# A quarter of one double weight tile loaded in fp32 over a second queue and cast on chip

## The chip, the cores and the metric

The kernel runs on one core of one Trainium2 chip. The time is device microseconds of a whole execution. The kernel before takes 436.98 us, the median of three runs (436.07 to 437.49).

The core has TensorE (PE; its weight loads are listed apart as PEld), VectorE (DVE), ScalarE (ACT), GpSimd (POOL) and SyncE (SP). Data moves between the chip's main memory and the on-chip memory of 128 partitions over 16 DMA engines, which are shared by the queues of SP and of POOL. A DMA issued from POOL's queue can change the type on the way (here fp32 to bf16); one issued from SP's queue moves the bytes as they are.

## The reference

Two layers follow one another. The first is a causal attention with a window of 128 and a bias that falls with distance, over 8 batches, 8 heads, 576 positions and 64 values a head. Its output `x` (8 x 576 x 512) goes into the second, which mixes in the spectrum:

```
X = np.fft.rfft(x, axis=1)
Xr, Xi = real and imaginary part of X[:, :64]
Yr = np.einsum('bmd,mde->bme', Xr, w_r) - np.einsum('bmd,mde->bme', Xi, w_i)
Yi = np.einsum('bmd,mde->bme', Xr, w_i) + np.einsum('bmd,mde->bme', Xi, w_r)
y = irfft of Y, which is zero outside the first 64 modes
u = x + y
out = u + np.maximum(u @ w_ch, 0.0)
```

For each of 64 modes there are two 512 x 512 fp32 matrices, one of `w_r` and one of `w_i`, of 1 MB each. Together they are most of what the kernel reads.

## The kernel before

**Two parts.** The first part (class `_Attention`) runs the attention of 16 units of one batch and four heads, in a fixed order of stages. While it runs, the first weights are fetched. The second part goes through the 64 modes in 16 groups `g` of four, and multiplies the eight batches' spectra (the stationary operand, columns of `XC`) with the modes' matrices (the moving operand, `wq`), L920. The order of the instructions of every engine is written out by hand: each engine does its work in the order in which the program emits it.

**Weights and turns.** A weight is numbered `i = 2 * mode + kind`, kind 0 for `w_r` and 1 for `w_i`. `turns` lists the order of use. Up to the last group a turn is two weights of the same kind and neighbouring modes, `[96, 98]` for example, which is `w_r` of modes 48 and 49. Of each matrix, partition `p` holds the four rows `4p` to `4p + 3`, which are 8 KB of fp32 in one run in main memory and become 4 KB of bf16 on chip.

**Loads.** All weights come over POOL's queue and are cast to bf16 by the DMA. The first 21, and eight more later, come one by one (`load_w`, L472). All others come as packs of two (`load_packs`). If both weights of the pack have the same kind, one DMA of 2 MB of fp32 brings them into a tile `[128, 2, 4, 512]` of bf16 (L491). In the last group a pack has both kinds of one mode, and comes in two or more DMAs (L499).

**Buffers and order.** Packs live in two pools of tiles with the tag `w`: the pool `w` with six buffers (`NWA // 2`) and, from position 40 on, the pool `w2` with two (`NWB // 2`). A pool hands its buffers out in rotation, and a load into a buffer waits until the matmuls that used it before are done. In the loop over `g` and `i`, the position is `k = 8 * g + i`. The position emits the eight matmuls of its turn (two weights by four row sets, L920), and after them the load of one more pack into the pool of the pack just used. Pack 96 and 98 is loaded after the turn at position 80 and used at position 96, the first of group 12. POOL issues its DMAs in order and waits before each for its buffer.

**Work beside it.** From group 8 on each position also emits a piece of side work: `project` (PE, with ACT's copies L715 and DVE's copy L692) or `augment` (PE, with a cast on ACT, L736, and one on DVE, L737). At the end of a group DVE scales the group's result (L608). After the last weight the kernel finishes the last modes and the token rows, and writes the output over SP's queue. Between 285 and 402 us SP issues no DMA.

Of the kernel before, what the change touches and what calls it, by code (L numbers as in the profile page):

```python
# [10 lines left out]
FP32 = mybir.dt.float32  # L11
BF16 = mybir.dt.bfloat16
# [8 lines left out]
P = 128  # L21
# [391 lines left out]
def kernel(  # L413
# [10 lines left out]
    nc = tc.nc  # L424
    ctx.enter_context(tc.manual_schedule(engines=ALL | {SP}))
    B, H, S, _ = q.shape
    NM, DM, _ = moe_w_r.shape
    AHEAD = {stage: 1 for stage in range(1, 14)}
    LATER = {12: 1, 13: 2, 14: 2, 15: 2}
    EARLY, NWA, NWB, AGAIN = 14, 12, 4, 8  # L430
    HM = NM // 2

    const = ctx.enter_context(tc.tile_pool(name="const", bufs=1))
    x = const.tile([P, B, FULL + 1, DM], BF16, name="x")
# [23 lines left out]
                      else [[2 * m], [2 * m + 1], [2 * m + 2], [2 * m + 3]])  # L458
    spot = {i: k for k, i in enumerate(i for turn in turns for i in turn)}
    turns[1].remove(1)  # L460
    wq, homes, todo_w, again = {}, {}, [i for turn in turns for i in turn], []

    def load_w(n, pool, chosen=None):
# [11 lines left out]
    def load_packs(n, pool):  # L475

        for _ in range(n):
            pack = [i for i in todo_w if i not in again][:2]
            if not pack:
                return  # L480
            assert len(pack) == 2
            t = pool.tile([P, 2, 4, DM], BF16, tag="w", name="w")
            kinds = {i % 2 for i in pack}
            for s, i in enumerate(pack):
                todo_w.remove(i)
                homes[i] = pool if s else False
                wq[i] = [t[:, s, a] for a in range(4)]
            m, w = pack[0] // 2, (moe_w_r, moe_w_i)
            if len(kinds) == 1:
                assert pack[1] == pack[0] + 2  # L490
                nc.gpsimd.dma_start(  # L491
                    out=t.rearrange("p s a e -> p s (a e)"),
                    in_=w[kinds.pop()][m : m + 2].rearrange("m (p a) e -> p m (a e)", a=4))
                continue
            for s, i in enumerate(pack):
                src = w[i % 2][i // 2].rearrange("(p a) e -> p a e", a=4)
                for part in ((slice(0, 4),) if i < 2 * NM - 1
                             else (slice(0, 2), slice(2, 3), slice(3, 4))):
                    nc.gpsimd.dma_start(out=t[:, s, part], in_=src[:, part])  # L499

    with ExitStack() as actx:
        at = _Attention(tc, actx, q, k, v, (ident, F, FT), x, XC, raw)
        n = len(at.units)
# [10 lines left out]
        pool = _Scratch(x[:, B - 2 :].rearrange("p b t c -> p (b t c)").bitcast(FP32))  # L514
# [55 lines left out]
    with ExitStack() as mctx:  # L570
        fix = mctx.enter_context(tc.tile_pool(name="fix", bufs=1))
        YT = fix.tile([P, 2, 4, B, HM, 2], BF16, name="YT")
        pool = mctx.enter_context(tc.tile_pool(name="fin", bufs=2))
        wctx = mctx.enter_context(ExitStack())
        wpool = wctx.enter_context(tc.tile_pool(name="w", bufs=NWA // 2, reuse_waits="tile"))
        again = todo_w[NWA : NWA + AGAIN]
        load_packs(NWA // 2, wpool)
        nc.gpsimd.memset(YT[:, 1, :, :, HM - 4 :], 0.0)
        lctx, pctx = ExitStack(), ExitStack()
# [261 lines left out]
        def finish_tokens(j):  # L841

            late_modes(yys[j][0], j, Z)
# [52 lines left out]
        for g in range(NM // 4):  # L896
# [5 lines left out]
            for i in range(8):  # L902
                k = 8 * g + i
                if i == 6 and g == LAST:
# [7 lines left out]
                    add_tokens(0)  # L912
                    finish_tokens(0)
                now = turns.pop(0) if turns and spot[turns[0][0]] == k else []
                for a in range(4):
                    for t in now:
                        m, ri = t // 2, t % 2
                        c0 = (a // 2 * 2 * NC + 16 * (1 - ri) + a % 2 * 8) * NM + m
                        into = part_acc if g == LAST and m < NM - 1 else acc
                        nc.tensor.matmul(  # L920
                            into[32 * (m % 4) : 32 * (m % 4) + 32],
                            lhsT=XC[:, c0 : c0 + 31 * NM + 1 : NM], rhs=wq[t][a],
                            start=(ri == 0 and a == 0), stop=(ri == (m > 0) and a == 3),
                            tile_position=(0, 32 * (m % 4)),
                        )
# [3 lines left out]
                if recycle:  # L929
                    load_w(1, early, [recycle.pop(0)])  # L930
                elif homes[own] not in (early, None, False):
                    load_packs(1, homes[own])
                if k == K1:
                    actx1.close()
                    w2 = mctx.enter_context(
                        tc.tile_pool(name="w2", bufs=NWB // 2, side="right", reuse_waits="tile")
                    )
                    load_packs(NWB // 2, w2)
                    right = mctx.enter_context(
                        tc.tile_pool(name="late", bufs=1, side="right", reuse_waits="tile")  # L940
# [8 lines left out]
                    for b in range(2):  # L949
                        nc.gpsimd.dma_start(  # L950
                            out=FM.rearrange("(k v) b s -> k v b s", v=16)[:, b, b],
                            in_=FT[64 * b + 56 : 64 * b + 64, b, : 2 * P],
# [125 lines left out]
```

## Time and profile before

| | before |
|---|---|
| median of three runs | 436.98 us |
| profiled execution | 436.75 us, span 435.0 us |
| PE busy | 314.1 us (72%), PEld 176.5 us |
| DVE, ACT, POOL busy | 184.8, 162.6, 94.3 us |
| POOL's DMA queue | 68.42 MB written, 78.1% of 16 engines' span |
| SP's DMA queue | 36.59 MB written, 25.3% |
| read and written in main memory | 162.53 MB and 9.44 MB |

The profile is one execution of the program. The span runs from the first to the last instruction that was recorded; the profiled execution took 1.75 us more than its span. The slices divide the span into 40 equal parts of 10.9 us, and a digit is a busy share in tenths. The row GB/s counts what the DMA engines wrote: a weight that is cast to bf16 on the way counts with half of what is read. The share of the DMA engines can be a little over 1, since a packet's recorded time overlaps that of the next one. "Idle before" is time in which an engine did nothing ahead of an instruction, with what ended it.

### The profile page before, as it was taken

How to read it: one execution, taken by the hardware profiler on the slowest of the kernel's cores; microseconds unless marked ns; L12 is line 12 of the kernel's file. 1: busy time of each engine (PE TensorE's matmuls, PEld its weight loads, DVE VectorE, ACT ScalarE, POOL GpSimd, SP SyncE). 2: the span in 40 equal slices, each digit the busy share in tenths (PEclk: the TensorE clock that was granted, in tenths of full speed). 3: DMA queues.
4: the chain of work that ended last, by engine and by line, in shares of the span. 5: the costliest groups of instructions: out<-in, count | busy, mean ns of one | idle time of the engine just before them, and what ended most of it. 6: DMA issues, size and time to landing. Idle time of an engine off the chain costs nothing.

```text
span 435.0 us, 7779 instructions
## 1 busy us (share of the span) xinstructions
PE 314.1 (72%) x3222; PEld 176.5 (41%) x3255; DVE 184.8 (42%) x333; ACT 162.6 (37%) x212; POOL 94.3 (22%) x176
## 2 busy tenths in 40 slices
PE   4589899978786535543442487888888999889893
PEld 3367677756665312111111133434343444334431
DVE  7789799978773301000000021331322233122684
ACT  6949899988780000000000012232231333201773
POOL 8701010103524002224112110111111111012600
PEclk9969999999999955555555569999998999899998
DMA  8999999999999999999999999999999999998598
GB/s 288 326 315 314 291 315 302 309 288 300 265 215 214 214 215 213 214 213 215 213 213 215 215 214 215 213 215 213 215 214 215 213 215 214 214 213 156 198 377 306
DMA packets 50483, 105.50 MB, mean 243 GB/s; under 512 B 4064, under 2 KB 21104, under 8 KB 50448
## 3 DMA queue, kind: packets, MB, share of 16 engines
q0 software_dynamic: 19472, 68.42, 78.1%
q1 hardware_dynamic: 30976, 36.59, 25.3%
q8 instruction: 25, 0.41, 0.4%
q14 instruction: 10, 0.08, 0.0%
HBM read 162.53 MB, written 9.44 MB: 395 GB/s over the span
## 4 chain that ended last, share of the span: by engine, by line
DMA 73%; PE 12%; DVE 6%; issue 3%; ACT 2%; SPq 1%; POOL 1%; DVEq 0%; ACTq 0%; POOLq 0%
DMA w<-in_moe_w_i_dram 37%; DMA w<-in_moe_w_r_dram 21%; DMA vr<-in_v_dram 8%; DMA kr<-in_k_dram 5%; PE av L344 2%; DMA qr<-in_q_dram 2%; DVE vb L246 2%; PE acc L920 1%; DVE o L877 1%; DVE x L360 1%; ACT att L307 1%; DVE att L318 1%; PE yy L788 1%; PE sc L297 1%; PE tp L263 1%
## 5 line engine op out<-in xcount | busy, mean ns | idle before, releaser
L920 PE MATMUL acc<-w,XC 128*32 128x512 bf16 x456 | 81.9, 486 | 69.9 <-DMA w<-in_moe_w_i_dram 35.0
L920 PEld LDWEIGHTS <-XC 128*32 128x32 bf16 x508 | 39.4, 148 | 111.6 <-issue 84.6
L307 ACT ACTIVATE att<-sc 128x1024 bf16<-128x1024 f32 x64 | 64.1, 1032 | 9.4 <-PE sc L297 9.4
L636 ACT CAST ZW<-zw 128x512 bf16<-128x512 f32 x8 | 4.7, 585 | 143.7 <-PE zw L634 143.7
L344 PE MATMUL av<-vb,att 128*128 128x132 bf16 (+1 forms) x576 | 38.4, 217 | 11.7 <-DVE x L360 7.1
L608 DVE TENSOR_SCALAR yq<-acc 128x512 bf16<-128x512 f32 x14 | 9.6, 687 | 81.9 <-PE acc L920 81.9
L344 PEld LDWEIGHTS <-att 128*128 128x128 bf16 x704 | 36.7, 98 | 17.1 <-DVE x L360 9.5
L709 PE MATMUL my<-wch,xT 128*128 128x512 bf16 x142 | 34.6, 386 | 6.0 <-ACT x L736 4.1
L715 ACT CAST XW<-my 128x512 bf16<-128x512 f32 x36 | 19.3, 589 | 51.8 <-PE my L678 42.6
L692 DVE COPY xT<-tr 128x1024 bf16<-128x1024 bf16 x18 | 12.5, 692 | 54.8 <-PE tr L689 54.8
L269 ACT COPY qkT<-tp 128x1152 bf16<-128x1152 bf16 x30 | 33.5, 1116 | 4.9 <-PE tp L263 4.3
L491 POOL DMA_DIRECT2D w<-in_moe_w_r_dram x22 | 15.6, 708 | 70.9 <-PE acc L920 45.2
L491 POOL DMA_DIRECT2D w<-in_moe_w_i_dram x23 | 16.3, 708 | 63.6 <-PE acc L920 47.6
L297 PE MATMUL sc<-qkT 64*64 64x256 bf16 (+2 forms) x640 | 25.3, 265 | 4.8 <-ACT qkT L269 1.2
L360 DVE TENSOR_TENSOR x<-av,rec 128x640 bf16<-128x640 f32 x32 | 26.4, 825 | 1.1
L709 PEld LDWEIGHTS <-xT 128*128 128x128 bf16 x144 | 13.5, 99 | 25.8 <-issue 9.7
L246 DVE CAST vb<-vr 64x1024 bf16<-64x1024 f32 x32 | 22.6, 707 | 0.2
L297 PEld LDWEIGHTS <-qkT 64*64 64x64 bf16 x640 | 14.6, 109 | 19.1 <-issue 16.0
L736 ACT CAST x<-my 128x512 bf16<-128x512 f32 x18 | 10.5, 585 | 30.0 <-PE my L678 18.2
L737 DVE CAST x<-my 128x512 bf16<-128x512 f32 x18 | 12.5, 692 | 21.8 <-PE my L678 21.8
L877 DVE TENSOR_TENSOR o<-yy,r 128x1024 f32<-128x1024 f32 (+1 forms) x21 | 20.7, 1018 | 2.3 <-ACT r L834 1.3
L318 DVE TENSOR_TENSOR att<-att,mask 128x1024 bf16<-128x1024 bf16 x32 | 20.5, 681 | 0.0
(144 smaller groups left out, 426.3 us busy)
## 6 DMA issues: line engine op xcount, KB each, us to landing
w<-in_moe_w_i_dram POOLq DMA_DIRECT2D x23, 1024.0 KB, 36.2
w<-in_moe_w_r_dram POOLq DMA_DIRECT2D x22, 1024.0 KB, 35.7
qr<-in_q_dram SPq DMA_DIRECT2D x16, 576.0 KB, 9.4
kr<-in_k_dram SPq DMA_DIRECT2D x16, 576.0 KB, 7.9
w<-in_moe_w_r_dram POOLq DMA_DIRECT2D x16, 512.0 KB, 14.1
vr<-in_v_dram SPq DMA_DIRECT2D x56, 128.0 KB, 7.7
w<-in_moe_w_i_dram POOLq DMA_DIRECT2D x13, 512.0 KB, 24.0
out_dram<-o SPq DMA_DIRECT2D x12, 512.0 KB, 4.2
```

The lines of the kernel that those rows point to most:

```text
L246: nc.vector.tensor_copy(self.vb[u % 2][row, :, :, :, W * half : W * half + D], src[row, :2])
L269: (self.nc.vector.tensor_copy if u < 2 and w == "q" else self.nc.scalar.copy)(dst.rearrange("q h (p j) -> q h p j", j=TPP), tp.rearrange(" ...
L297: nc.tensor.matmul(sc[64 * half : 64 * half + 64, e, j * 256 + c0 : j * 256 + c0 + n], lhsT=qkT[row, 1, h, k0 + j : k0 + P : 2], rhs=qkT[r ...
L307: self.nc.scalar.activation(self.att[u % 2][:, kt * 8 * P : (kt + 1) * 8 * P], sc.rearrange("p e n -> p (e n)"), AF.Exp, scale=1.0 / math. ...
L318: nc.vector.tensor_tensor(out=rows, in0=rows, in1=self.table[:, heads], op=ALU.mult)
L344: nc.tensor.matmul(bank[:, qt * W : qt * W + rhs[j].shape[1]], lhsT=att[:, o : o + P], rhs=rhs[j], start=(n == 0 and j == 0), stop=(n == l ...
L360: nc.vector.tensor_tensor(out=self.x[:, b, :, cs].rearrange("p t (h d) -> p h t d", h=2), in0=tiles[:, :, :, :D], in1=rec.unsqueeze(-1).br ...
L491: nc.gpsimd.dma_start(out=t.rearrange("p s a e -> p s (a e)"), in_=w[kinds.pop()][m : m + 2].rearrange("m (p a) e -> p m (a e)", a=4))
L709: nc.tensor.matmul(mm, lhsT=xT[:, n, dt], rhs=wch[:, dt], start=(dt == 0), stop=False, skip_group_check=True)
L715: nc.scalar.copy(XW[:, j, n], mms[n])
L877: nc.vector.tensor_tensor(out=whole(o, c), in0=part(yy, c), in1=whole(r, c), op=ALU.add)
L920: nc.tensor.matmul(into[32 * (m % 4) : 32 * (m % 4) + 32], lhsT=XC[:, c0 : c0 + 31 * NM + 1 : NM], rhs=wq[t][a], start=(ri == 0 and a == 0 ...
```

## The change

One pack, 96 and 98, is loaded in another way. POOL's DMA brings partitions 0 to 95 as before, in bf16. For partitions 96 to 127, each of the two weights gets a tile of its own from the same pool (a whole buffer, taken as fp32, of which 32 partitions are used). SP's queue brings its 32 rows of 8 KB in four transfers of 8 partitions. ACT casts the rows of the first weight into the pack's tile, and DVE those of the second. The casts are emitted right before the pack's matmuls.

```diff
+    PIECES = 2 * (3 * NM // 4)
...
+    casts = []
...
             if len(kinds) == 1:
                 assert pack[1] == pack[0] + 2
-                nc.gpsimd.dma_start(
-                    out=t.rearrange("p s a e -> p s (a e)"),
-                    in_=w[kinds.pop()][m : m + 2].rearrange("m (p a) e -> p m (a e)", a=4))
+                n = P - 32 if pack[0] == PIECES else P
+                src = w[kinds.pop()][m : m + 2].rearrange("m (p a) e -> p m (a e)", a=4)
+                nc.gpsimd.dma_start(out=t.rearrange("p s a e -> p s (a e)")[:n], in_=src[:n])
+                for s in range(2 if n < P else 0):
+                    raw_w = pool.tile([P, 2, 4, DM], BF16, tag="w", name="w")
+                    raw_w = raw_w.rearrange("p s a e -> p (s a e)").bitcast(FP32)
+                    for o in range(n, P, 8):
+                        nc.sync.dma_start(out=raw_w[o : o + 8], in_=src[o : o + 8, s])
+                    casts.append((t[n:, s].rearrange("p a e -> p (a e)"), raw_w[n:]))
                 continue
...
                 now = turns.pop(0) if turns and spot[turns[0][0]] == k else []
+                if PIECES in now:
+                    nc.scalar.copy(*casts[0])
+                    nc.vector.tensor_copy(*casts[1])
                 for a in range(4):
```

`PIECES` is 96, since `NM` is 64.

## The prediction

> **What bounds the kernel now.** I read the page's slices first, for the stage the change sits in; then the windows over that stage, the waits in it, the chain that ended last, and the timeline where the changed tile is used.
>
> ```profile
> PE   4589899978786535543442487888888999889893
> DMA  8999999999999999999999999999999999998598
> GB/s 288 326 315 314 291 315 302 309 288 300 265 215 214 214 215 213 214 213 215 213 213 215 215 214 215 213 215 213 215 214 215 213 215 214 214 213 156 198 377 306
> ...
> 296.00:330.00 34.00, 28.18 (x189) 13.95 (x190) 9.07 (x15) 9.37 (x17) 4.21 (x6) 1.00 1.06 214
> 330.00:376.00 46.00, 41.39 (x252) 18.50 (x258) 13.32 (x24) 12.78 (x23) 6.03 (x10) 0.96 1.06 214
> ...
> 295.23 37.72 DMA w<-in_moe_w_i_dram
> 335.22 37.07 DMA w<-in_moe_w_i_dram
> 372.58 24.25 DMA w<-in_moe_w_i_dram
> ```
>
> From slice 12 to slice 36 the transfer engines never pause and write 214 GB/s of bf16, so read 428 GB/s of fp32. The windows (columns: length, then PE, PEld, DVE, ACT and POOL busy, clock, DMA share, GB/s) show PE close behind them, 28.2 of 34.0 us and 41.4 of 46.0 us busy. The chain is weight transfers up to 396.83, and from there a tail of some 38 us that hangs on the last ones. So an edit is worth what it does to the landing of the last weight pieces (396.8 to 401.84 us).
>
> The trace also keeps each DMA's sixteen completions, one for each transfer engine, and each packet's duration. The last weight DMA's completions stand, before the last of them at 401.84: eight early ones at -3.68, -3.67, -3.63, -3.55, -3.53, -3.51, -2.83 and -2.59 us, then eight late ones at -1.32 to 0. These gaps hold from load to load, moved only by single jumps of about 1.1 us, one engine at a time, each beside a 16 KB packet of the instruction queue. So it is the late eight that set the end, and the others have 2.6 us to spare.
>
> A packet of 8 KB read takes 324 ns and follows the one before by 305 ns: a 2 MB pack is 16 packets on each engine, 16 x 305 = 4.88 us, the distance between landings (323.23, 328.11, 332.95).
>
> **The change part by part.** *Fewer partitions through POOL's queue.* The pack of modes 48 and 49 (real part) brings 96 of 128 partitions, two rows each: 12 packets an engine instead of 16, -4 x 305 = -1.22 us on all sixteen.
>
> *Eight transfers through SP's queue.* SP issues nothing between 285 and 403 us, so nothing is queued behind its waits; an issue costs it 0.37 to 0.75 us. Each carries 8 rows of 8 KB, 64 packets in all. If they spread over all sixteen engines, +1.22 us each and the sum is zero. With 8 rows a transfer can occupy eight engines: those get eight packets, +2.44, net +1.22 us; the other eight stay at -1.22. If the eight are the early ones, the last landing goes from 0 to the later of -1.22 (late half) and -2.59 + 1.22 = -1.37: 1.22 us earlier. If they are the late ones, 1.22 us later. The Trainium skill (DMA: Bandwidth & Descriptors, Why a DMA increments its semaphore by 16 and not by 1) says that a hardware-queue transfer of 8 rows takes the lowest-numbered eight engines; no run here shows which number the early ones have. The nearest row is POOL's first 8-row transfer (into FM, 226.2 to 227.9 us): its eight packets ran on six of the early and two of the late engines. So I take the early half as the likelier, and keep both ends; with two late engines among the eight (those at -0.95 and -1.29) the last landing would go to -0.95 + 1.22 = +0.27.
>
> *What those transfers cost at the far end.* This is the term I weigh most. They write whole fp32 rows into 8 neighbouring partitions, eight engines at once. The nearest row is the tail of v, 32 partitions (64 to 95) written by sixteen engines, 512 bytes a packet. Where all 128 partitions are written, such a packet takes a mean of 29.9 ns (8.0 to 10.0 us, 1020 packets); in the tail that follows (10.25 to 11 us, 51 packets) 53.0 ns, 1.77 times as long, and again in the next unit (from 30 to about 50). So writing into a quarter of the partitions already slows the packet. Here it is a sixteenth, with packets sixteen times as big. Below: no slowing, 0 us. The tail's own factor: 325 x 0.77 x 8 packets = 2.0 us more on each of the eight engines. The factor twice over, since the partitions are 4 times fewer and the engines half: 3.1, so 325 x 2.1 x 8 = 5.5 us. Above: strictly in turn by four, with the late half's own writes between, 325 x 3.5 x 8 = 9.1 us. I take 5.0 us, near the doubled factor, because 64 KB in one burst is less easily absorbed than the tail's 2 KB a partition. Then the burdened half ends at -2.59 + 1.22 + 5.0 = +3.6 us. The Trainium skill (SBUF — State Buffer, Door 1: The DMA port swizzle) has the rule for this: bandwidth depends on how many of 16 ports the partitions reach, and 8 neighbours reach two. By its 27.2 GB/s a port, an estimate from the page, 64 KB need 1.2 us, 0.9 more than a packet, 7.2 us over eight; the sum would then be +5.8 us instead of +3.6. The tail's packets agree in direction.
>
> *Two more buffers.* Each raw tile takes a whole buffer of the six in pool w. In rotation they are the next two, those of the two packs used after the one just freed, so the SP transfers start when those are used up: about 295.2 and 300.1 us. The pack behind gets the third next buffer, so its load and all behind it in POOL's queue wait for four more uses.
>
> ```profile
> 305.46 0.70 POOL L491 DMA_DIRECT2D w<-in_moe_w_i_dram  x1 [4.64 <-PE acc L920]
> ...
> 323.63 1.08 PE L920 MATMUL acc<-w,XC 128*32 128x512 bf16 x8
> 328.29 1.07 ACT L715 CAST XW<-my 128x512 bf16<-128x512 f32 x2 [2.19 <-PE my L678]
> 328.84 1.09 PE L920 MATMUL acc<-w,XC 128*32 128x512 bf16 x8
> 328.95 0.69 DVE L692 COPY xT<-tr 128x1024 bf16<-128x1024 bf16 x1 [2.53 <-PE tr L689]
> 329.56 0.68 DVE L608 TENSOR_SCALAR yq<-acc 128x512 bf16<-128x512 f32 x1
> 332.99 1.93 PE L920 MATMUL acc<-w,XC 128*32 128x512 bf16 x8 [1.21 <-DMA w<-in_moe_w_i_dram]
> ...
> 377.23 1.79 PE L920 MATMUL acc<-w,XC 128*32 128x512 bf16 x8 [1.18 <-DMA w<-in_moe_w_r_dram]
> ...
> w<-in_moe_w_i_dram POOLq DMA_DIRECT2D x23, 1024.0 KB, 36.2
> ```
>
> Loads land 36.2 us after issue, 7.4 packs of 4.88 us. With issues held for four uses the queue still has three packs (14 us) when it is fed again, at about 314.8 us, and POOL does nothing else there. I cost this at nothing; its cover is that depth. It goes if the packs in hand land later than PE uses them, which it cannot outrun.
>
> *The two casts* stand in program order right before the pack's matmuls (328.84, 8 matmuls). On ACT the cast follows L715's copies, which end at 329.36; by L307's 1032 ns for 1024 elements and L715's 589 for 512, 2048 elements are 1.92 us: done 331.3. On DVE it follows L608, which ends at 330.24; by L246's 707 ns for 1024, about 1.4: done 331.65. So the matmuls start some 2.5 us late, and after such an idle PE runs slow, as at 332.99 and 377.23, where 1.2 us of idle are followed by eight matmuls in 1.9 and 1.8 us instead of 1.09. Before, that slow stretch came one pack later, after 1.21 us of idle which now go too; netted, PE is about 1.5 us behind at 337. It has 1.18 us of idle at 377.23 and the slow stretch after it (some 1.7 us) to take that up in, before the pieces that matter. I cost it at nothing, 1.5 us if that slack is gone.
>
> **Sum.** -1.22 (fewer rows) +2.44 (eight packets) +5.0 (crowded writes) on the burdened half, which had 2.59 to spare: last landing +3.6, tail unchanged. The profiled execution took 436.75 us (span 435.0 and 1.75 around it), 0.23 below the median 436.98, inside the runs' spread: 440.3 us.
>
> **The rivals.** *Crowded writes, the forecast* (0.46): for it, the tail's 53 against 30 ns; against it, the single 1 KB packets patched into eight neighbours near 404.4 us take 46 to 78 ns, hardly longer than alone (46 to 53). Its own range runs from the tail's single factor to the upper bound: 437.4 to 444.5.
>
> *It balances the two halves* (0.36): the writes are absorbed, the early eight take the load, and the last landing moves by -1.22: 435.5. For it, the eight-and-eight split and a shift of 2 x 1.22 = 2.44 for a gap of 2.59. It decides as long as the slowing x of a packet stays small: the burdened half ends at -1.37 + 8x, so the gain is whole up to 0.02 us and gone at 0.17 us.
>
> *The eight engines are the late ones, or partly, or the transfers spread over all sixteen* (0.10): without crowding +1.2, +0.3 or 0, so 438.0 at the full price and 436.75 at none. The Trainium skill (DMA: Bandwidth & Descriptors, Issuing engines are not separate DMA queues) says that all queues share the same sixteen engines, by which a second queue alone gains nothing; the trace's DMA share of 1.06 in both windows agrees that no engine time is free.
>
> *The casts' stall is not taken up* (0.08): +1.5 us, 438.3. Against it, the idle at 377.23.
>
> **How the numbers follow.** A change within 0.3% (1.3 us around 436.98: 435.67 to 438.29) is about what cannot be told from none. The forecast's case is slower but for its lowest end (0.44 and 0.02); the balancing case straddles the line, 0.28% below the profiled time and 0.33% below the median (faster 0.22, same 0.14); the engines' case is half same, half slower; the stall's nearly all slower (0.07). Faster 0.22, same 0.22, slower 0.56. The range must reach the balancing case: 435.3 to 444.5; above lies the stricter crowding, below nothing that I can name.
>
> **What would show it.** Right: completions of the packs landing from 300 to 315 us spread wider than 3.5 us, with packets of the SP queue well above 325 ns; the last weight landing near 405.4 us. Balanced instead: the last DMA's sixteen completions within about 2.5 us, landing near 400.6. Casts: PE idle of about 2.5 us before the pack's matmuls, whatever the sum. Buffers: a POOL gap from about 293 to 315 us, with DMA share still at 1.06; a dip there would mean that the queue ran dry. I am wrong if SP's 8 KB packets take 305 to 340 ns.

## The result and the profile after

The changed kernel takes 442.39 us, the median of six runs, against 436.69 us of the kernel before: a ratio of 1.0135 with a 95% interval of 1.0106 to 1.0164, so 5.7 us more. The forecast was 440.3 us, in a range of 435.3 to 444.5. The profiled execution took 442.13 us, with a span of 440.4.

The slices of the page after (40 equal parts of the span; digits are busy tenths, and GB/s is what the DMA engines wrote):

```profile
PE   4679899978786445534433377986687999869894
DMA  8999999999999999999999999999999999997598
GB/s 282 329 314 324 294 303 295 313 283 305 251 213 214 214 214 214 213 214 214 215 211 214 215 214 215 214 215 181 191 214 214 214 215 213 214 213 151 176 378 318
```

The row DMA still shows nines where the weights stream. Only the row below tells the loss: two slices, the 28th and 29th, write 181 and 191 GB/s where 214 or 215 stand on both sides. The engines were busy and moved less.

The windows over that stretch, of the kernel before and of the changed one (columns: length, then PE, PEld, DVE, ACT and POOL busy, clock, DMA share, GB/s):

```profile
296.00:304.00 8.00, 6.38 (x45) 3.32 (x44) 1.38 (x2) 2.15 (x5) 0.70 (x1) 1.00 1.06 215
304.00:312.00 8.00, 7.02 (x52) 3.23 (x50) 3.17 (x6) 2.24 (x5) 1.40 (x2) 1.00 1.06 215
312.00:325.00 13.00, 10.31 (x68) 5.31 (x69) 2.77 (x4) 3.32 (x6) 1.41 (x2) 1.00 1.06 213
```

```profile
296.00:304.00 8.00, 6.38 (x42) 3.25 (x42) 1.38 (x2) 1.86 (x4) 0.00 (x0) 1.00 1.16 187
304.00:312.00 8.00, 5.75 (x30) 2.35 (x28) 1.38 (x2) 1.46 (x3) 0.00 (x0) 0.79 1.25 163
312.00:325.00 13.00, 7.64 (x58) 4.50 (x59) 3.17 (x6) 2.73 (x5) 0.71 (x1) 1.00 1.06 214
```

The share rises from 1.06 to 1.16 and 1.25 while the bytes fall: packets lie on the engines longer, and more of them at once. From 312 us share and bytes are as before. SP issues its eight transfers at 295.2 to 296.6 and at 300.2 to 301.5 us.

The bytes of the 20 us from 296 to 316 us by queue (packets, MB written, share of the engines; q0 is POOL's queue, q1 SP's), of the kernel before and of the changed one:

```profile
q0 software_dynamic: 1107, 4.27, 106.0%
```

```profile
q0 software_dynamic: 809, 3.12, 97.5%
q1 hardware_dynamic: 128, 0.52, 19.9%
```

POOL's queue reads twice what it writes, so 6.24 + 0.52 = 6.76 MB were read. The kernel before wrote 4.27 MB here, so read 8.54. The missing 1.78 MB are 4.2 us at the 0.427 MB/us of the kernel before, and that is a mean over all sixteen engines. The last weight lands at 407.30 us instead of 401.84, 5.46 us later, and the span is 5.4 us longer. The prediction's first sign is there too: the sixteen completions of the two loads that land from 300 to 315 us spread over 4.4 and 6.5 us, against some 3.5 in the kernel before.

The trace's packet records of SP's queue show where that comes from. These are the durations in ns of its 64 packets of 8 KB, in order of time, eight to a line, so one line for about each transfer:

```
322 322 322 322 322 322 322 322
748 804 808 812 675 642 611 634
1095 1022 954 818 691 669 627 642
1106 1056 1026 1005 951 722 713 786
322 322 322 322 322 322 322 322
951 928 759 671 612 539 506 526
1018 941 753 678 616 534 509 520
1025 941 756 684 622 542 504 514
```

The first transfer of each weight takes 322 ns a packet, about as every 8 KB read of the kernel before (324). The three behind it take 504 to 1106 ns, and the mean over all is 647. In the same stretch POOL's 4 KB packets (8 KB read) slow from a mean of 324 ns to 396 (296 to 304 us) and 484 (304 to 312 us).

### The profile page after: what moved, and what is told of

Read it like the earlier page. It is cut to its first block, busy times and chain, and to the rows that moved or that the text cites. A ratio compares the mean times of both kernels' runs of the same rounds, so it can differ in the third digit from the quotient of the medians.

```text
span 440.4 us, 7800 instructions
## 1 busy us (share of the span) xinstructions
PE 313.4 (71%) x3222; PEld 176.5 (40%) x3255; DVE 186.2 (42%) x334; ACT 164.5 (37%) x213; POOL 93.8 (21%) x176
## 4 chain that ended last, share of the span: by engine, by line
DMA 65%; PE 17%; DVE 6%; issue 5%; ACT 3%; SPq 1%; POOL 1%; another core or an unknown queue 1%; DVEq 0%; POOLq 0%; ACTq 0%
DMA w<-in_moe_w_i_dram 30%; DMA w<-in_moe_w_r_dram 10%; DMA wch<-in_moe_w_ch_dram 8%; DMA vr<-in_v_dram 6%; DMA qr<-in_q_dram 4%; PE my L717 3%; DMA qr<-in_moe_w_i_dram 2%; PE av L344 2%; PE acc L931 2%; DMA vr<-in_moe_w_r_dram 2%; DVE vb L246 1%; PE my L686 1%; DVE o L885 1%; ACT XW L723 1%; PE tp L263 1%
## 5 line engine op out<-in xcount | busy, mean ns | idle before, releaser
L931 PE MATMUL acc<-w,XC 128*32 128x512 bf16 x456 | 80.5, 478 | 77.4 <-DMA w<-in_moe_w_i_dram 37.8
```

The lines of the kernel that those rows point to most:

```text
L931: nc.tensor.matmul(into[32 * (m % 4) : 32 * (m % 4) + 32], lhsT=XC[:, c0 : c0 + 31 * NM + 1 : NM], rhs=wq[t][a], start=(ri == 0 and a == 0 ...
```

## The experiments

The theory at this point: the packets are slow because eight engines write into 8 neighbouring partitions at once. The rivals: that eight engines alone carry the load, whatever they write; that PE starts late behind the casts; that the transfers read badly; that the buffers starve POOL's queue. Each time below is a median, and each ratio is to the kernel before, measured beside it on the same chip.

### Partitions 4 apart instead of neighbours

```diff
-                    for o in range(n, P, 8):
-                        nc.sync.dma_start(out=raw_w[o : o + 8], in_=src[o : o + 8, s])
+                    for o in range(n, n + 4):
+                        nc.sync.dma_start(out=raw_w[o:P:4], in_=src[o:P:4, s])
```

> The changed kernel, but each of the eight SP transfers carries 8 partitions that lie 4 apart (96, 100, ... 124, then 97, 101, ...) instead of 8 neighbours. Bytes, rows, number of transfers and the casts stay. If the crowding is in the place that a transfer writes to (8 neighbours at once), the later SP packets fall from 500 to 1100 ns to below 450 ns, the loads on the other eight engines are slowed less, and the time falls from 442.4 us to 435.5 to 438. If it is the eight engines themselves (eight packets for each, whatever they write), or two queues taking turns on an engine, the packets stay at 500 ns and more and the time at 441 to 443.5 us. If the late PE start behind the casts is the cause, the time also stays.

Measured: 438.14 us against 437.64, ratio 1.0018 (0.9995 to 1.0041). All 64 packets take 309 to 322 ns, and the time is just above the expected 435.5 to 438. Its windows and its bytes from 296 to 316 us:

```profile
296.00:304.00 8.00, 6.43 (x45) 3.39 (x44) 1.38 (x2) 2.12 (x4) 0.00 (x0) 1.00 1.06 231
304.00:312.00 8.00, 6.37 (x47) 3.34 (x44) 2.67 (x4) 2.27 (x5) 0.00 (x0) 1.00 1.07 228
```

```profile
q0 software_dynamic: 1035, 3.99, 99.1%
q1 hardware_dynamic: 128, 0.52, 6.9%
```

The share is back at 1.06, the higher GB/s comes from SP's fp32, which is written at full width, and 7.98 + 0.52 = 8.50 MB were read, as good as the 8.54 of the kernel before. With the same bytes, the same number of rows in a transfer and the same casts, the slowdown is gone. So neither the eight engines nor the second queue nor the casts made it.

### The low quarter, 4 apart

Partitions 0 to 31 come over SP, POOL brings 32 to 127.

```diff
-                n = P - 32 if pack[0] == PIECES else P
+                n = 32 if pack[0] == PIECES else 0
...
+                    for o in range(4):
+                        nc.sync.dma_start(out=raw_w[o:n:4], in_=src[o:n:4, s])
```

> Like the one with a step of 4, but the quarter that comes over SP is partitions 0 to 31 and POOL brings 32 to 127. If crowding by the place of writing is the cause and partitions 96 to 127 are shared with the writes of the engines that set the end, this takes the SP packets to 322 to 340 ns, leaves the late engines with four packets less, and the time falls to 435.0 to 436.5 us, so 0.2 to 1.7 us below the kernel before. If the place does not matter beyond the neighbours, it equals the run with partitions 96 to 127 in steps of 4 within 0.5 us. If the eight engines or the casts are the cause: 441 to 443.5 us.

Measured: 437.79 us, ratio 1.0006 (0.9980 to 1.0031), packets at 309 to 322 ns. The place of the quarter makes no difference that can be told, and the gain that was possible by balance (1.2 us) did not come, though nothing is crowded.

### One transfer of 32 rows

```diff
-                    for o in range(n, P, 8):
-                        nc.sync.dma_start(out=raw_w[o : o + 8], in_=src[o : o + 8, s])
+                    nc.sync.dma_start(out=raw_w[n:], in_=src[n:, s])
```

> The changed kernel, but each weight's 32 rows come in one SP transfer of 32 partitions instead of four of 8. If such a transfer spreads over all sixteen engines, each has two packets of a weight and the sum of packets is that of the kernel before. Crowding by place: 32 partitions, so a slowing like the tail of v (1.3 to 1.8 times), 4 packets an engine, 0.4 to 1 us: 437 to 438.5 us. No crowding: 436.4 to 437.0. Casts and buffers as the cause: 441 to 443.5.

Measured: 437.93 us, ratio 1.0011 (0.9983 to 1.0039). The 64 packets take 346 ns in the mean, nine of them over 400, the longest 460. That lies between 322 and 647, but it is only 1.07 times 322, less than the 1.3 to 1.8 times that the tail of v had let expect, and too little to be seen in the time. The trace is of an execution of 441.67 us, most of whose excess lies ahead of these transfers: the load before them lands at 297.74 us, in the kernel before at 293.79.

### Reading and writing apart

The step of 4 had changed what is written and what is read. Two kernels change one of them each. In both the rows of the quarter land in permuted order, so the product is not that of the layer. The lines below stand in the place of the changed kernel's loop over `o`.

```diff
 e9:  for j in range(4):
          nc.sync.dma_start(out=raw_w[n + 8 * j : n + 8 * j + 8], in_=src[n + j : P : 4, s])
 e10: for j in range(4):
          nc.sync.dma_start(out=raw_w[n + j : P : 4], in_=src[n + 8 * j : n + 8 * j + 8, s])
```

Reading 4 apart, writing neighbours:

> The step of 4 changed two things at once: the partitions that a transfer writes and the rows that it reads, which were one run of 64 KB in main memory and became 8 KB pieces 32 KB apart. Here only the reading has the step of 4; the writing goes to 8 neighbours, as in the change. The 32 rows of each weight so land in permuted order and the product is not that of the layer. If crowding is in the writing: later SP packets at 500 to 1100 ns and 441.5 to 443.5 us, a ratio of 1.010 to 1.014. If it is in the reading of one run of 64 KB by eight engines: packets at 322 ns and 437.4 to 438.3 us.

Measured: 443.54 us against 437.36, ratio 1.0157 (1.0119 to 1.0195), a little over the expected 1.010 to 1.014, packets at 647 ns in the mean, 48 of 64 over 400. Its windows are close to those of the changed kernel:

```profile
296.00:304.00 8.00, 6.43 (x40) 3.17 (x39) 1.39 (x2) 1.66 (x3) 0.00 (x0) 1.00 1.15 190
304.00:312.00 8.00, 4.33 (x24) 1.77 (x23) 0.69 (x1) 1.07 (x2) 0.00 (x0) 0.68 1.27 166
```

Reading one run of 64 KB, writing 4 apart:

> The other half of the same test: the writing goes to 8 partitions 4 apart, the reading is one run of 64 KB as in the change (rows again permuted). If crowding is in the writing: packets at 322 ns and 437.4 to 438.3 us, ratio 0.999 to 1.003. If in the reading: 500 to 1100 ns and 441.5 to 443.5 us.

Measured: 437.75 us, ratio 1.0009 (0.9989 to 1.0029), packets at 309 to 322 ns:

```profile
296.00:304.00 8.00, 6.43 (x47) 3.33 (x46) 1.38 (x2) 2.22 (x5) 0.00 (x0) 1.00 1.07 235
304.00:312.00 8.00, 6.78 (x50) 3.30 (x48) 3.07 (x6) 2.17 (x5) 0.00 (x0) 1.00 1.06 226
```

The price is in the place of writing alone.

### Partitions 2 apart

```diff
-                    for o in range(n, P, 8):
-                        nc.sync.dma_start(out=raw_w[o : o + 8], in_=src[o : o + 8, s])
+                    for o in (n, n + 1, n + 16, n + 17):
+                        nc.sync.dma_start(out=raw_w[o : o + 15 : 2], in_=src[o : o + 15 : 2, s])
```

> The changed kernel with transfers of 8 partitions that lie 2 apart (96, 98, ... 110 and so on), so that two and not four engines write into each run of four neighbours. If crowding goes by runs of four neighbouring partitions, the later SP packets lie between the 322 ns of the step of 4 and the 500 to 1100 ns of neighbours, at 380 to 600 ns, and the time between too: 438.3 to 440.3 us. If only directly neighbouring rows crowd each other, the packets are at 322 ns and the time within 0.5 us of the run with a step of 4 (438.1). If any 16 near partitions do, it is as slow as the changed kernel (442 to 443.5).

Measured: 439.55 us against 437.38, ratio 1.0050 (1.0033 to 1.0067), between the two. The trace kept of it is of an execution of 598.7 us, far from the median, so the packets are read from one more execution:

> The step of 2 once more, for its packets, since the execution profiled before was disturbed (598.7 us against 439.3 to 439.6 of the others). By the theory of runs of four neighbours: the first eight packets 322 ns, the later ones 380 to 600 ns, mean below 500, and about half of the change's loss of bytes between 296 and 316 us.

Measured: 439.16 us beside 437.0. The first transfer of each weight has packets at 322 ns and the later ones run to 689 (600 were expected at most); the mean is 461, between 322 and 647. The bytes from 296 to 316 us:

```profile
q0 software_dynamic: 988, 3.82, 97.1%
q1 hardware_dynamic: 128, 0.52, 13.4%
```

7.64 + 0.52 = 8.16 MB were read, 0.38 less than before, or 0.9 us over all engines, where the change lost 4.2. I had expected about half of the loss, and it is a fifth; the time lost is 2.2 us of some 5.6. Of these 2.2 us the traced execution had lost 1.4 ahead of the changed transfers (the load before them lands at 295.22 us instead of 293.79). Part of the crowding goes when two engines and not four share a run of four partitions, and the rest goes at one. The loss falls faster than the number of sharers; the law between the two is not settled by three points.

### One weight's rows only

```diff
-                for s in range(2 if n < P else 0):
+                if n < P:
+                    nc.gpsimd.dma_start(out=t[n:, 1].rearrange("p a e -> p (a e)"),
+                                        in_=src[n:, 1])
+                for s in range(1 if n < P else 0):
...
-                    nc.vector.tensor_copy(*casts[1])
```

> The changed kernel, but only the first of the pack's two weights brings its 32 rows over SP, in four transfers of 8 neighbours, with one raw tile and ACT's cast; POOL brings the rows of the second in a transfer of 32 partitions of its own. Half the crowded writes. If each crowded transfer has its price, about half of the 5.7 us: 439.2 to 440.5 us. If one late engine pays a fixed price, or if the waits for two buffers make it, 441.5 to 443.5. If the second weight's transfers were hidden behind the first's, the same 441.5 to 443.5.

Measured: 439.56 us, ratio 1.0051 (1.0032 to 1.0069): 2.2 us, within the expected half. Between 296 and 316 us, 3.69 MB by POOL and 0.26 by SP make 7.64 MB read, 0.90 MB missing, half of the change's 1.78. The crowded transfers add up; none hides behind another.

### Half the tile, uncrowded

```diff
-                n = P - 32 if pack[0] == PIECES else P
+                n = 64 if pack[0] == PIECES else 0
...
+                    for o in (0, 1, 2, 3, 32, 33, 34, 35):
+                        nc.sync.dma_start(out=raw_w[o : o + 29 : 4], in_=src[o : o + 29 : 4, s])
```

> Uncrowded (8 partitions 4 apart), but 64 of the 128 partitions come over SP (0 to 63), in sixteen transfers. The eight engines of SP's transfers get 16 packets more and 8 fewer from POOL, +2.44 us; the other eight have 8 fewer, -2.44 us. If the eight still had time to spare after a quarter (they were the early ones), the time falls or stays: 435.5 to 437.5. If one of them already sets the end after a quarter, as the equal times of the two kernels with a step of 4 suggest, each further packet counts in full: 1.2 us above the quarter, 438.8 to 440.0 us.

Measured: 438.98 us, ratio 1.0053 (1.0026 to 1.0080), all 128 packets at 309 to 322 ns. That is 1.6 us above the kernel before, and no gain. It is what was expected if one of the eight engines sets the end already after a quarter, so that what they get further counts. The intervals of the quarter (0.9980 to 1.0031) and of the half are wide against the 1.2 us between them, so the times alone do not show it; the completions below bear it out.

### The casts one turn earlier

```diff
-                if PIECES in now:
+                if PIECES - 3 in now:
                     nc.scalar.copy(*casts[0])
                     nc.vector.tensor_copy(*casts[1])
```

> The changed kernel, with the two casts emitted one turn earlier (before the matmuls of weights 93 and 95). The idle of 2.42 us before the pack's matmuls goes or falls below 0.5 us. If the end is set by the transfers alone, as I priced it, the time stays at 441.5 to 443.3 us. If PE's late start is carried to the end, it falls by 1.5 to 2.5 us, to 440 to 441.

Measured: 443.17 us, ratio 1.0118 (1.0092 to 1.0144), where the change has 1.0135 and, in the run again below, 1.0127. The timeline of the changed kernel (start, length, engine, line, in brackets the idle before) shows the stall:

```profile
329.34 1.07 ACT L723 CAST XW<-my 128x512 bf16<-128x512 f32 x2 [2.19 <-remote]
335.68 1.89 ACT L924 CAST w<-w 32x2048 bf16<-32x2048 f32 x1
335.86 0.68 DVE L616 TENSOR_SCALAR yq<-acc 128x512 bf16<-128x512 f32 x1
336.57 1.22 DVE L925 CAST w<-w 32x2048 bf16<-32x2048 f32 x1
337.63 1.66 PE L931 MATMUL acc<-w,XC 128*32 128x512 bf16 x8 [2.42 <-ACT w L924]
```

and that of the kernel with early casts shows it gone:

```profile
330.99 1.89 ACT L924 CAST w<-w 32x2048 bf16<-32x2048 f32 x1
331.28 1.22 DVE L925 CAST w<-w 32x2048 bf16<-32x2048 f32 x1
336.24 1.09 PE L931 MATMUL acc<-w,XC 128*32 128x512 bf16 x8
```

The idle of 2.42 us is gone and the time has not moved. Yet the chain that ended last, of the changed kernel, names the cast:

```profile
281.41 43.12 DMA w<-in_moe_w_r_dram
335.68 1.90 ACT w L924
337.63 1.66 PE acc L931 x8
359.19 33.27 DMA w<-in_moe_w_i_dram
392.75 14.55 DMA w<-in_moe_w_i_dram
```

Between the pieces shown, work of PE and ACT goes on up to 359.19 us, where the chain reaches the issue of a load that lands 33 us later. It got there because that load was issued when PE was done with a buffer. But the DMA share from 330 to 376 us is 1.06, as before, so the load lay behind others in a queue that never ran dry, and I take it that an earlier issue would not have brought it earlier. The early casts left the time unchanged; so a chain that passes through an issue into such a queue does not say that the work before the issue costs time.

### The change again

> The changed kernel once more, beside the others on the same chip: 442 to 443.5 us, 4 to 5 us above the step of 4, with the later SP packets at 500 to 1100 ns. If its place was an accident of one execution, the packets of this one differ by more than a third.

Measured: 442.91 us against 437.38, ratio 1.0127 (1.0108 to 1.0146). 48 of the 64 packets are again over 400 ns, the mean is 648 (647 the first time), and 3.10 MB by POOL were written from 296 to 316 us.

### The smallest uncrowded version

The rows 0 to 31 of one weight only, 4 apart, its cast one turn earlier.

```diff
...
+                if n:
+                    nc.gpsimd.dma_start(out=t[:n, 1].rearrange("p a e -> p (a e)"),
+                                        in_=src[:n, 1])
+                for s in range(1 if n else 0):
...
+                    for o in range(4):
+                        nc.sync.dma_start(out=raw_w[o:n:4], in_=src[o:n:4, s])
...
+                if PIECES - 3 in now:
+                    nc.scalar.copy(*casts[0])
```

> The candidate that takes what the runs allow: rows 0 to 31 of the first weight alone over SP in steps of 4, one raw tile, its cast one turn earlier; POOL brings the rest. The eight engines get 2 packets more on balance, the other eight 2 fewer: 0.6 us either way. If the eight still have that much to spare: -0.6 us, a ratio of 0.998 to 0.999. If one of them is among those that set the end: 0 to +0.6 us, 1.000 to 1.002. I expect no difference that can be told, 436.8 to 438.0.

Measured: 437.42 us against 437.36, ratio 1.0000 (0.9983 to 1.0018). No version here beats the kernel before.

## Why the prediction was right

**Crowded writes** were the forecast and are what happened. With the writing alone spread the ratio falls to 1.0009, with the reading alone spread it stays, at 1.0157. The row that carried the forecast, the tail of v with 53 against 30 ns, pointed the right way, but its factor of 1.77 for 32 partitions did not come back: one transfer into 32 partitions had packets 1.07 times as long. The 1 KB patches that spoke against it may have been too small to show it: here, too, the first transfer of each weight went through at 322 ns.

**The size** was too small: the last landing was forecast 3.6 us later and came 5.46 later. What failed is the step "5.0 us more on each of the eight engines", which charged the burdened half alone, and 0.63 us a packet where the mean was 0.33. Summed over the packets, SP's are longer by (647 - 322) x 8 = 2.6 us an engine, and POOL's packets on all sixteen engines by (396 - 324) x 302 + (484 - 324) x 254 packets, over 16, = 3.9 us. The slowing of the other queue, which the sum left out, was the larger part. With both, the burdened half would end at -2.59 + 1.22 + 2.6 + 3.9 = +5.1, an estimate, since recorded packet times overlap; measured are 5.46. The late half also fell back, which the sum had at -1.22: fourteen of the sixteen completions of the last weight come at 403.16 us or later, after the last one of the kernel before at 401.84. That the time still lay in the range was in part luck, for one term was too large and the other missing.

The completions separate two effects. They are counted from the load that lands near 294 us, ahead of the changed transfers, to the last weight, once for the mean of the sixteen and once for the last of them (us, one execution each):

| kernel | mean | last |
|---|---|---|
| before | 108.10 | 108.05 |
| the change, and again | 112.27, 112.57 | 113.23, 113.72 |
| neighbours, reading 4 apart | 112.31 | 113.35 |
| 4 apart: high quarter, low quarter, writing only | 108.18, 108.22, 108.23 | 108.72, 108.56, 109.42 |
| half the tile, 4 apart | 108.49 | 110.44 |
| 2 apart | 109.02 | 109.41 |

In the change the mean loses 4.2 to 4.5 us, by bytes it was 4.2, and with the writes 4 apart it loses 0.1: this part is the crowding. The last engine loses 5.2 to 5.7 us in the change and still 0.5 to 1.4 with the quarter uncrowded, which fits the unequal load of the engines.

The estimate from a figure of the Trainium skill (SBUF — State Buffer, Door 1: The DMA port swizzle) gave 0.9 us more for a packet and +5.8 us for the sum. The total is close to the 5.46 us by which the last weight came later, but not by its parts: an SP packet was 0.33 us longer in the mean, and the rest came over POOL's packets. The rule of the Trainium skill that four neighbours share a port agrees with all three steps: 4 apart 321 ns in the mean, 2 apart 461, neighbours 647.

**The balance** (0.36) fell, and not through crowding alone: the uncrowded kernels should have gained 1.2 us and stand at 1.0006 to 1.0018. The step that failed is the 2.59 us to spare, read off one execution (of the load that lands at 401.22 us; at the last one it is 2.55). The last engine of the half tile is later by 2.4 us, that of the quarter by 0.5 to 1.4, at nearly the same mean, so after a quarter some of the eight engines most likely set the end. Moreover the distances differ between executions: at the load that lands near 264 us, ahead of any changed transfer, the earliest engine is 2.5 us ahead of the last in the kernel before, 3.6 in the changed one, 1.6 with the one transfer of 32 rows and 2.3 with the early casts. A fixed shift cannot be fitted to that. The numbers of the early engines were not seen in any run; that stays open.

**Two more buffers** at nothing: right. POOL's issues stop and go on in the changed kernel at

```profile
292.07 0.65 POOL L495 DMA_DIRECT2D w<-in_moe_w_r_dram  x1 [4.63 <-PE acc L931]
322.69 0.71 POOL L495 DMA_DIRECT2D w<-in_moe_w_i_dram  x1 [29.97 <-issue]
```

later than the forecast 314.8. In the kernels with a step of 4 they go on at 318.1 to 318.7, so some 3.6 us of the difference are not from crowding, and the rest is that the packs in between came late. The share in the window from 312 to 325 us is 1.06, so the queue did not run dry. The three kernels with a step of 4 also take the two buffers and lose nothing that can be told.

**The casts** at nothing: right, and their sizes too: 1.89 us for 1.92 on ACT, 1.22 for 1.4 on DVE, 2.42 us of idle for 2.5. Taking the idle away gained nothing. Less sure than it sounded is that PE runs slow after an idle: in the changed kernel eight matmuls take 1.66 us after those 2.42 us, but 1.08 us after 2.03 us of idle at 387.60 us.

## What to carry to other kernels

In these runs a transfer's cost depended on where it writes. Before a load is cut into pieces of few neighbouring partitions, look whether several engines then write into the same four, and if so give each piece partitions that lie 4 apart, or bring the rows in one transfer (32 rows: 346 ns a packet, no loss that can be told). In a stage where the DMA engines never pause (a share of 1.06 here), read the GB/s beside it: packets that crowd each other raised the share to 1.25 while the bytes fell from 215 to 163 GB/s. And before a fixed imbalance between engines is mended, read it in several executions.

## What the runs showed that was not expected

The first transfer of each four goes through at full speed (eight packets at 322 ns, single ones at 326 to 418) and only the ones behind it are slow, in all traces of kernels that write in transfers of 8 neighbours, and in the one read for 2 apart. It looks as if 64 KB were taken up before the engines are held back; by what, no run shows.

The slow writes hold back the other queue as well: POOL's packets went from 324 to 484 ns in the mean. Beside the same 0.52 MB on the second queue, the first wrote 3.12 MB in those 20 us where it wrote 3.99 with the places 4 apart.
